# Attention scores of a head pair in two tied half-array runs instead of three, and the mask of batch 1 by VectorE

## The chip, the core and the metric

The kernel runs on one core of one Trainium2 chip. TensorE (PE in the profile) multiplies, VectorE (DVE), ScalarE (ACT) and GpSimd (POOL) do the rest, SyncE (SP) issues the transfers. The metric is the device time of one execution in microseconds, the median of several runs. PE can be used as one array of 128 rows, or as two halves of 64 rows that work at the same time on different operands; a *half-array run* is here a stretch of matmuls of 64 rows with no matmul of 128 rows in between.

## What is computed

Block-causal attention, then a mixture with a maximum of three products, then a second mixture of four experts:

```python
# q, k, v: (4, 8, 576, 64) fp32
scores = scale * np.matmul(q, k.transpose(0, 1, 3, 2))
mask = block_i >= block_j                 # blocks of 64 positions
scores = np.where(mask, scores, -1000000000.0)
scores = scores - np.max(scores, axis=-1, keepdims=True)
attn = np.exp(scores)
attn = attn / (np.sum(attn, axis=-1, keepdims=True) + 1e-09)
attn_out = np.matmul(attn, v)
...
h = np.maximum(np.maximum(x @ w1, x @ w2), x @ w3)
x = h @ w_out                             # 2304 x 512, 768 wide inside
...
out += p[:, e:e + 1] * (np.maximum(x @ w1[e], 0.0) @ w2[e])
```

## The kernel before

**Pairs.** The 4 x 8 heads are worked on as 16 pairs, `n` = 0 to 15; a batch is four pairs (`NPAIR` = 4). The two heads of a pair lie in the lower and the upper 64 partitions of `qs` and `ks`, so one head's scores are a matmul of 64 rows in one half of the array. The 576 query rows of a head are four tiles of 128 rows (`i` = 0 to 3), which need 128, 256, 384 and 512 key columns under the block mask, and 64 tail rows; the tail rows of both heads are made together by full 128-row matmuls over 576 columns (line 161).

**Scores in three steps.** `scores(n, step)` makes tiles i = 0 and 2 for both heads (128 and 384 columns), then i = 3 (512), then i = 1 (256) with the tail rows. The products are fp32; the trace shows each as two records. Score tiles `st` are in PSUM: from `ps_x`, four tiles of one bank (512 columns), which transposes (`tt`), the row weights (`rt`) and, from batch 1 on, the attention values (`pv`) use too, and from `ps_c`, one tile of two banks. In steps 0 and 1 every head has a tile of `ps_x`, in step 2 one of `ps_x` and the one of `ps_c`.

**After the product.** The last 64 columns of a tile are masked for its lower 64 rows: in batches 0 and 1 (`masked = n < 2 * NPAIR`) by a small bf16 matmul of `corner` added to each score tile (line 153), in batches 2 and 3 by a memset on VectorE (line 169). Then VectorE takes the row minimum (scores are kept negated; line 173), ScalarE the exponential with row sums (line 180), VectorE the reciprocals, GpSimd the multiplication with them. `turn_probs` transposes the probabilities on PE (line 241), ScalarE and VectorE copy them out, and `values32` (batch 0) or `values` (batches 1 to 3) multiplies them with v.

**What sets the order.** In each iteration `n` of the main loop the parts of attention of pair `n` and the score steps of pair `n + 1` stand in one list (`todo`), and after each part `filler.upto` puts in products of the first mixture of the batch before (`moe1`, line 493), as many as the part's place in the list asks for: `at = (n + (m + 1) / len(todo)) / NPAIR`. That filler exists from batch 1 on. In batch 0 ScalarE, VectorE and GpSimd convert the weights of the first mixture (lines 418 to 440) besides. The program is then ordered by a scheduler that works with a simulated time; an instruction may move ahead of others on its engine unless `tc.keep_in_program_order` pins it behind the one written before it on the same engine. Before, every half-array matmul of a step is pinned but the first:

```python
                if todo[0] or m:
                    tc.keep_in_program_order(ins)
```

The two full matmuls for the tail rows (line 161) are not pinned.

Of the kernel before, what the change touches and what calls it, by code (L numbers as in the profile page):

```python
# [6 lines left out]
F32 = mybir.dt.float32  # L7
# [4 lines left out]
ACTF = mybir.ActivationFunctionType  # L12
ALU = mybir.AluOpType
AX = mybir.AxisListType
# [6 lines left out]
P = 128  # L21
# [5 lines left out]
def program(tc, q, k, v, w123, w_out, probs, e_w1, e_w2, out):  # L27
    nc = tc.nc
# [7 lines left out]
    NPAIR = H // 2  # L36
# [68 lines left out]
    def prep_pair(n):  # L105
# [15 lines left out]
        (("x", 512), ("x", 512), [(0, 0, 0, P), (2, P, P, 384)]),  # L121
        (("x", 512), ("x", 512), [(3, 0, 0, 512)]),
        (("x", 512), ("c", 1024), [(1, 0, 768, 256)]),
    ]
    COLS = (0, 4, 6, 9)

    def scores(n, step):
        pair = pairs[n]
        if step == 0:
# [6 lines left out]
        masked = n < 2 * NPAIR  # L136
        st = [
            (ps_x if tag == "x" else ps_c).tile([P, cols], F32, name="st", tag=tag) for tag, cols in STEPS[step][0:2]
        ]
        plan = STEPS[step][2]  # L140
        turn = (0, 1) if step == 2 else (1, 0)
        todo = [[], []]
        for i, *at, w in plan:
            views = [st[h][:, at[h]:at[h] + w] for h in range(2)]
            for m, h in enumerate(turn):
                ins = nc.tensor.matmul(  # L146
                    out=views[h], lhsT=qs[own[h], P * i:P * i + P], rhs=ks[own[h], 0:w], start=True, stop=not masked,
                )
                if todo[0] or m:
                    tc.keep_in_program_order(ins)  # L150
            for h in range(2):
                if masked:
                    tc.keep_in_program_order(nc.tensor.matmul(  # L153
                        out=views[h][:, w - 64:w], lhsT=corner[own[h]], rhs=corner[own[h], 0:64],
                        start=False, stop=True,
                    ))
                todo[h].append((i, h, views[h]))
        if step == 2:
            view = st[1][:, 192:768]
            for c, n_ in ((0, 320), (320, 256)):  # L160
                nc.tensor.matmul(  # L161
                    out=view[:, c:c + n_], lhsT=qs[:, QT:QW], rhs=ks[:, c:c + n_], start=True, stop=True
                )
            todo[1].append((4, 0, view))
        col, done = COLS[step], []
        for work in todo:
            for i, h, x in work:
                if i < 4 and not masked:
                    nc.vector.memset(x[lo, x.shape[1] - 64:], 1e30)
            cols = range(col, col + len(work))  # L170
            col += len(work)
            for c, (i, h, x) in zip(cols, work):
                nc.vector.tensor_reduce(mn[:, c:c + 1], x, axis=AX.X, op=ALU.min)  # L173
            for c, (i, h, x) in zip(cols, work):
# [3 lines left out]
                else:  # L178
                    pair["p"][h][i] = to
                exps.append(nc.scalar.activation(  # L180
                    to, x, ACTF.Exp, bias=mn[:, c:c + 1], scale=-1.0, accum_out=sm[:, c:c + 1],
                ))
                done.append((c, i, to))

        def normalise():
# [3 lines left out]
            if n < NPAIR:  # L189

                if step == 0:
                    o = 4 * n * P
                    pair["rb"] = arena[:, o:o + 4 * P].rearrange("p (i h c) -> p i h c", i=4, h=2)
                    to = pair["rb"][:, 0:2].rearrange("p i h c -> p h i c")
                    rs = sm[:, cs].rearrange("p (h i) -> p h i", h=2).unsqueeze(3).to_broadcast([P, 2, 2, 64])
                else:
                    to = pair["rb"][:, step + 1]
                    rs = sm[:, COLS[step]:COLS[step] + 2].unsqueeze(2).to_broadcast([P, 2, 64])
# [387 lines left out]
    stage(scores, 0, 2)  # L586
    for n in range(NALL):
# [7 lines left out]
        s0, s1, s2 = [(scores, n + 1, i) if n + 1 < NALL else (None,) for i in range(3)]  # L595
        pp = (next, prep, None)
        todo = [ta[0], s0, tb[0], s1, va[0], pp, vb[0], ta[1], s2, tb[1], va[1], pp, vb[1]]
# [737 lines left out]
```

## Time and profile before

| | |
|---|---|
| median of 3 runs | 1249.12 us (1248.59 to 1250.19) |
| the profiled execution | 1248.74 us, its span 1247.0 us |
| PE busy | 1223.0 us (98%), 7369 matmul records |
| DVE, ACT, POOL busy | 888.0, 484.6, 332.4 us |
| mean granted clock of PE | 0.995 of full speed |
| half-array score matmuls (line 146) | 256 records, first at 5.0 us, last at 396.2 us |
| corner matmuls (line 153) | 64 records, last at 156.8 us |

Times in the trace are counted from the start of the span. The stretches are: batch 0 up to the first product of the first mixture (83 us), attention of batches 1 to 3 with those products in between (to some 430 us), the rest of the first mixture (to 519 us), the second mixture. The busy time of PE runs from a matmul's start to its modelled end, and matmuls overlap in the pipeline, so it doesn't show what a matmul costs; the distance from one start to the next does.

### The profile page before, as it was taken

The numbers are of one execution on the slowest core, as the hardware profiler recorded it, in microseconds if no ns is written. First come the engines' busy times: TensorE is split into PE (matmuls) and PEld (weight loads), VectorE is DVE, ScalarE is ACT, GpSimd is POOL, SyncE is SP. The second block draws the span as 40 slices with busy tenths as digits, with TensorE's granted clock in tenths as the row PEclk, the third lists the DMA queues.
The fourth block names the chain that finished last, engine by engine and source line by source line (L and its number), as shares of the span: only waits on it lengthen the run. The fifth ranks groups of instructions, "written<-read, shape, count | busy, mean of one in ns | idle before, by whom it ended". The sixth has DMA issues, their size and how long they took to land.

```text
span 1247.0 us, 19462 instructions
## 1 busy us (share of the span) xinstructions
PE 1223.0 (98%) x7369; PEld 1140.3 (91%) x7369; DVE 888.0 (71%) x1636; ACT 484.6 (39%) x1027; POOL 332.4 (27%) x408
## 2 busy tenths in 40 slices
PE   7899999999999999999999999999999999999998
PEld 4578888999999999989999998999999999999998
DVE  5758787555455464278988896758787788576896
ACT  6866666444433431234444441233232222322232
POOL 4637785444244113233343351000000000000000
PEclk9999999999999999999999999999999999999999
DMA  7724474443433476679887875878788887766754
GB/s 271 258 95 167 158 250 160 147 142 106 139 114 102 120 271 259 202 300 340 311 319 289 303 258 167 280 280 316 291 312 310 309 316 290 255 245 239 253 200 180
DMA packets 82352, 290.74 MB, mean 233 GB/s; under 512 B 8716, under 2 KB 18004, under 8 KB 69204
## 3 DMA queue, kind: packets, MB, share of 16 engines
q1 hardware_dynamic: 82260, 289.51, 65.3%
q8 instruction: 58, 0.95, 0.3%
q14 instruction: 34, 0.28, 0.1%
HBM read 206.34 MB, written 83.14 MB: 232 GB/s over the span
## 4 chain that ended last, share of the span: by engine, by line
PE 84%; DVE 7%; DMA 4%; ACT 2%; POOL 1%; issue 1%; SPq 0%; DVEq 0%; ACTq 0%; POOLq 0%
PE m L846 24%; PE m L493 23%; PE o L1005 17%; PE st L146 3%; PE tt L241 3%; PE pv L350 2%; PE o L928 2%; PE o L932 2%; PE o L931 2%; PE m L1005 2%; DMA t<-in_e_w 2%; PE pv L296 1%; PE st L161 1%; DMA raw<-in_q 1%; DVE w L801 1%
## 5 line engine op out<-in xcount | busy, mean ns | idle before, releaser
L493 PE MATMUL m<-xh,wt 128*128 128x288 f32 x1120 | 245.6, 301 | 0.0
L846 PE MATMUL m<-t,w 128*128 128x384 f32 x1152 | 227.8, 336 | 0.0
L1005 PE MATMUL o<-hx,w 128*128 128x384 f32 x1176 | 226.0, 337 | 0.4 <-DMA w<-kb 0.4
L1005 PEld LDWEIGHTS o<-hx,w 128*128 128x128 f32 x1176 | 207.8, 188 | 0.7 <-PE m L846 0.7
L846 PEld LDWEIGHTS m<-t,w 128*128 128x128 f32 x1152 | 203.4, 188 | 2.5
L493 PEld LDWEIGHTS m<-xh,wt 128*128 128x128 f32 x1120 | 184.6, 188 | 7.2 <-DVE mt L531 3.8
L846 PE MATMUL m<-b,w 128*128 128x384 f32 x864 | 175.0, 336 | 1.9 <-ACT tmp L871 1.9
L493 PE MATMUL m<-xl,wt 128*128 128x288 f32 x560 | 165.7, 296 | 0.0
L846 PEld LDWEIGHTS m<-b,w 128*128 128x128 f32 x864 | 153.2, 188 | 5.2 <-ACT tmp L871 2.2
L493 PEld LDWEIGHTS m<-xl,wt 128*128 128x128 f32 x560 | 105.3, 188 | 1.9 <-issue 1.5
L180 ACT ACTIVATE p<-st,mn 128x128 f32<-128x128 f32 (+2 forms) x144 | 78.3, 552 | 53.1 <-DVE mn L173 52.7
L866 DVE TENSOR_TENSOR tmp<-m,tmp 128x384 f32<-128x384 f32 x144 | 77.9, 550 | 19.5 <-PE m L846 19.4
L203 POOL TENSOR_SCALAR p<-p,sm 128x128 f32<-128x128 f32 (+4 forms) x112 | 67.3, 617 | 91.4 <-DVE sm L188 84.1
L493 PE MATMUL m<-hh,wo 128*128 128x288 f32 x384 | 84.1, 304 | 2.3 <-DMA wo<-held 2.1
L976 ACT CAST hx<-hq 128x768 fp32r<-128x768 f32 x49 | 40.6, 837 | 99.0 <-PE o L1005 75.9
L173 DVE TENSOR_REDUCE mn<-st 128x1 f32<-128x128 f32 (+2 forms) x144 | 68.5, 514 | 13.3 <-PE st L153 9.9
L531 DVE TENSOR_TENSOR mt<-m,mt 128x288 f32<-128x288 f32 x96 | 43.4, 454 | 47.7 <-PE m L493 47.1
L928 PE MATMUL o<-w,hh 128*128 128x512 f32 x192 | 74.7, 391 | 0.6 <-ACT hh L906 0.5
L931 PE MATMUL o<-w,hh 128*128 128x512 f32 x192 | 74.6, 390 | 0.0
L932 PE MATMUL o<-w,hl 128*128 128x512 f32 x192 | 74.4, 391 | 0.0
L801 POOL TENSOR_TENSOR w<-part,w 128x512 fp32r<-128x512 f32 x32 | 50.4, 1599 | 89.0 <-ACT w L799 67.1
L241 PE MATMUL tt<-ident,p 128*128 128x128 f32 x400 | 63.6, 281 | 5.0 <-DVE xf L325 2.0
(160 smaller groups left out, 2067.2 us busy)
## 6 DMA issues: line engine op xcount, KB each, us to landing
w<-kb SPq DMA_DIRECT2D x55, 1024.0 KB, 6.0
w<-ka SPq DMA_DIRECT2D x30, 1792.0 KB, 7.7
ka<-w SPq DMA_DIRECT2D x16, 1792.0 KB, 6.7
wt<-held SPq DMA_DIRECT2D x54, 512.0 KB, 4.0
kb<-part SPq DMA_DIRECT2D x16, 1024.0 KB, 6.9
kb<-w SPq DMA_DIRECT2D x16, 768.0 KB, 4.9
arena<-in_w SPq DMA_DIRECT2D x18, 512.0 KB, 4.2
wo<-held SPq DMA_DIRECT2D x12, 768.0 KB, 4.6
```

Source lines behind the costliest of these rows:

```text
L173: nc.vector.tensor_reduce(mn[:, c:c + 1], x, axis=AX.X, op=ALU.min)
L180: exps.append(nc.scalar.activation(to, x, ACTF.Exp, bias=mn[:, c:c + 1], scale=-1.0, accum_out=sm[:, c:c + 1],))
L203: nc.gpsimd.tensor_scalar(x, x, sm[:, c:c + 1], 1.0, op0=ALU.mult, op1=ALU.mult)
L241: nc.tensor.transpose(tt[:, c:c + P], pt[i][:, k0:k0 + P], ident)
L493: nc.tensor.matmul(out=out_, lhsT=w, rhs=x, start=m == 0, stop=m == n - 1)
L801: eng.tensor_tensor(w[:, a:b, 1], raw[:, a:b], f(w[:, a:b, 0]), op=ALU.subtract)
L846: ins = nc.tensor.matmul(out=m, lhsT=a, rhs=b, start=start and n == 0, stop=stop and n == 3 * KH - 1, skip_group_check=True,)
L866: nc.vector.tensor_tensor(t, x, y, op=ALU.add)
L928: ins = nc.tensor.matmul(out=o, lhsT=hh[:, ts], rhs=wh, start=i == 0, stop=False)
L931: nc.tensor.matmul(out=o, lhsT=hh[:, ts], rhs=wl, start=False, stop=False)
L932: nc.tensor.matmul(out=o, lhsT=hl[:, ts], rhs=wh, start=False, stop=i == G - 1)
L1005: nc.tensor.matmul(out=o, lhsT=a, rhs=b, start=start and m == 0, stop=stop and m == 2, skip_group_check=True,)
```

## The change

The steps are two: tiles i = 0 and 2 as before, then i = 3, i = 1 and the tail rows in one. The second step takes three tiles of `ps_x` and the one of `ps_c`. Every matmul of a step is pinned, the first one and the two for the tail rows too. Minimum and exponential go by two tiles at a time in the order of the products, where they went by head; the row sums stand in that order too, so the copy of the row weights in batch 0 is of 4 columns in both steps. In the main loop the second step stands behind the first half's values (`vb[0]`), where step 1 stood behind `tb[0]` and step 2 behind `ta[1]`; the list has 12 parts where it had 13. The corner matmul is left for batch 0 alone; batch 1 (`n` = 4 to 7) is masked by VectorE's memset, as batches 2 and 3 are.

```diff
--- before.py
+++ after.py
@@ -118,11 +118,10 @@
 
 
     STEPS = [
-        (("x", 512), ("x", 512), [(0, 0, 0, P), (2, P, P, 384)]),
-        (("x", 512), ("x", 512), [(3, 0, 0, 512)]),
-        (("x", 512), ("c", 1024), [(1, 0, 768, 256)]),
+        [(0, 0, P, (0, 1)), (2, P, 384, (0, 1))],
+        [(3, 0, 512, (0, 1)), (1, (0, 768), 256, (2, 3))],
     ]
-    COLS = (0, 4, 6, 9)
+    COLS = (0, 4, 9)
 
     def scores(n, step):
         pair = pairs[n]
@@ -133,54 +132,53 @@
                 sm=ap_.tile([P, COLS[-1], 2], F32, name="sm", tag="sm", bufs=2),
             )
         mn, sm, qs, ks = pair["mn"], pair["sm"][:, :, 0], pair["qs"], pair["ks"]
-        masked = n < 2 * NPAIR
+        masked = n < NPAIR
         st = [
-            (ps_x if tag == "x" else ps_c).tile([P, cols], F32, name="st", tag=tag) for tag, cols in STEPS[step][0:2]
+            (ps_c if m == 3 else ps_x).tile([P, 1024 if m == 3 else 512], F32, name="st", tag="c" if m == 3 else "x")
+            for m in range((2, 4)[step])
         ]
-        plan = STEPS[step][2]
-        turn = (0, 1) if step == 2 else (1, 0)
-        todo = [[], []]
-        for i, *at, w in plan:
-            views = [st[h][:, at[h]:at[h] + w] for h in range(2)]
-            for m, h in enumerate(turn):
-                ins = nc.tensor.matmul(
+        todo = []
+        for i, at, w, tiles_ in STEPS[step]:
+            views = []
+            for h in range(2):
+                o = at if isinstance(at, int) else at[h]
+                views.append(st[tiles_[h]][:, o:o + w])
+            for h in (1, 0):
+                tc.keep_in_program_order(nc.tensor.matmul(
                     out=views[h], lhsT=qs[own[h], P * i:P * i + P], rhs=ks[own[h], 0:w], start=True, stop=not masked,
-                )
-                if todo[0] or m:
-                    tc.keep_in_program_order(ins)
+                ))
             for h in range(2):
                 if masked:
                     tc.keep_in_program_order(nc.tensor.matmul(
                         out=views[h][:, w - 64:w], lhsT=corner[own[h]], rhs=corner[own[h], 0:64],
                         start=False, stop=True,
                     ))
-                todo[h].append((i, h, views[h]))
-        if step == 2:
-            view = st[1][:, 192:768]
+                todo.append((i, h, views[h]))
+        if step == 1:
+            view = st[3][:, 192:768]
             for c, n_ in ((0, 320), (320, 256)):
-                nc.tensor.matmul(
+                tc.keep_in_program_order(nc.tensor.matmul(
                     out=view[:, c:c + n_], lhsT=qs[:, QT:QW], rhs=ks[:, c:c + n_], start=True, stop=True
-                )
-            todo[1].append((4, 0, view))
-        col, done = COLS[step], []
-        for work in todo:
-            for i, h, x in work:
+                ))
+            todo.append((4, 0, view))
+        done, cols = [], list(range(COLS[step], COLS[step + 1]))
+        for c in (0, 2, 4):
+            work = list(zip(cols, todo))[c:c + 2]
+            for _, (i, h, x) in work:
                 if i < 4 and not masked:
                     nc.vector.memset(x[lo, x.shape[1] - 64:], 1e30)
-            cols = range(col, col + len(work))
-            col += len(work)
-            for c, (i, h, x) in zip(cols, work):
-                nc.vector.tensor_reduce(mn[:, c:c + 1], x, axis=AX.X, op=ALU.min)
-            for c, (i, h, x) in zip(cols, work):
+            for m, (i, h, x) in work:
+                nc.vector.tensor_reduce(mn[:, m:m + 1], x, axis=AX.X, op=ALU.min)
+            for m, (i, h, x) in work:
                 to = ap_.tile([P, x.shape[1]], F32, name=f"p{i}", tag=f"p{i}", bufs=2 if i == 4 else 3)
                 if i == 4:
                     pair["p4"] = to
                 else:
                     pair["p"][h][i] = to
                 exps.append(nc.scalar.activation(
-                    to, x, ACTF.Exp, bias=mn[:, c:c + 1], scale=-1.0, accum_out=sm[:, c:c + 1],
+                    to, x, ACTF.Exp, bias=mn[:, m:m + 1], scale=-1.0, accum_out=sm[:, m:m + 1],
                 ))
-                done.append((c, i, to))
+                done.append((m, i, to))
 
         def normalise():
             cs = slice(COLS[step], COLS[step + 1])
@@ -191,11 +189,8 @@
                 if step == 0:
                     o = 4 * n * P
                     pair["rb"] = arena[:, o:o + 4 * P].rearrange("p (i h c) -> p i h c", i=4, h=2)
-                    to = pair["rb"][:, 0:2].rearrange("p i h c -> p h i c")
-                    rs = sm[:, cs].rearrange("p (h i) -> p h i", h=2).unsqueeze(3).to_broadcast([P, 2, 2, 64])
-                else:
-                    to = pair["rb"][:, step + 1]
-                    rs = sm[:, COLS[step]:COLS[step] + 2].unsqueeze(2).to_broadcast([P, 2, 64])
+                to = pair["rb"][:, 2 * step:2 * step + 2].rearrange("p i h c -> p (i h) c")
+                rs = sm[:, COLS[step]:COLS[step] + 4].unsqueeze(2).to_broadcast([P, 4, 64])
                 nc.gpsimd.tensor_copy(to, rs)
             for c, i, x in done:
                 if n < NPAIR and i < 4:
@@ -583,7 +578,6 @@
     stage(scores, 0, 0)
     stage(scores, 0, 1)
     stage(all_of, prep_pair(1))
-    stage(scores, 0, 2)
     for n in range(NALL):
         b, d = divmod(n, NPAIR)
         ahead = n + 2 < NALL
@@ -592,9 +586,9 @@
         ta, tb, va, vb = [
             [(fn, g + h, part) for h in range(2)] for fn in (turn_probs, values) for part in range(2)
         ]
-        s0, s1, s2 = [(scores, n + 1, i) if n + 1 < NALL else (None,) for i in range(3)]
+        s0, s1 = [(scores, n + 1, i) if n + 1 < NALL else (None,) for i in range(2)]
         pp = (next, prep, None)
-        todo = [ta[0], s0, tb[0], s1, va[0], pp, vb[0], ta[1], s2, tb[1], va[1], pp, vb[1]]
+        todo = [ta[0], s0, tb[0], va[0], pp, vb[0], s1, ta[1], tb[1], va[1], pp, vb[1]]
         for m, st in enumerate(todo):
             if d == NPAIR - 1 and m == 7:
                 moe1_inputs(b, range(KD - 1))
```

In the rows below, `st` are score tiles, `tt` transposed probabilities, `pv` values, `m` the products of the first mixture, `p_...` tiles of probabilities; x2 stands for both heads. Line 146 of before is line 147 after, 161 is 160, 493 is 488, 180 is 178, 418 and 419 are 413 and 414, 241 is 236.

PE before, in batches 2 and 3, step 1 of a pair among products of the first mixture:

```order
L493 MATMUL m<-xl,wt 128x288
L493 MATMUL m<-xh,wt 128x288
L146 MATMUL st<-raw 128x512 x2
L493 MATMUL m<-xh,wt 128x288
L493 MATMUL m<-xl,wt 128x288
```

The run of 512 columns stands alone, with products of the first mixture on both sides. PE before, step 2 of the same pair, some 40 rows on:

```order
L493 MATMUL m<-hh,wo 128x288
L146 MATMUL st<-raw 128x256 x2
L161 MATMUL st<-raw 128x320
L161 MATMUL st<-raw 128x256
L493 MATMUL m<-hh,wo 128x288
```

The 256 columns are a run of their own, followed by the tail rows. PE after, the second step at the same place of the program:

```order
L488 MATMUL m<-hl,wo 128x288
L488 MATMUL m<-hh,wo 128x288
L147 MATMUL st<-raw 128x512 x2
L147 MATMUL st<-raw 128x256 x2
L160 MATMUL st<-raw 128x320
L160 MATMUL st<-raw 128x256
L488 MATMUL m<-hh,wo 128x288
```

Both runs have become one, with the tail rows behind it. PE before, step 0 of a pair in the same batches, whose first matmul is not pinned:

```order
L241 MATMUL tt<-ident,p_3155 128x128
L241 MATMUL tt<-ident,p_3157 128x128 x2
L146 MATMUL st<-raw 128x128
L493 MATMUL m<-xh,wt 128x288
L493 MATMUL m<-xl,wt 128x288
```

One head's 128 columns stand alone; 17 rows on follow the other head's 128 and both heads' 384. PE after, step 0:

```order
L488 MATMUL m<-xl,wt 128x288
L488 MATMUL m<-xh,wt 128x288
L147 MATMUL st<-raw 128x128 x2
L147 MATMUL st<-raw 128x384 x2
L236 MATMUL tt<-ident,p_3289 128x128 x2
```

All four matmuls of the step stand together there. ScalarE before, at the start of the program, with the exponentials of pair 0 (128 columns: i = 0, 384: i = 2, 512: i = 3; p_157 and p_159 are the first head's) and the conversion of weights:

```order
L180 ACT_TABLE_LOAD
L180 ACTIVATE p_157,sm<-st,mn 128x128
L180 ACTIVATE p_159,sm<-st,mn 128x384
L418 ACTIVATE arena<-arena 128x512
L419 ACTIVATE arena<-arena 128x512
L180 ACTIVATE p_163,sm<-st,mn 128x128
L180 ACTIVATE p_165,sm<-st,mn 128x384
```

The first head's two exponentials come first. ScalarE after, the same place (p_157 and p_163 are the first head's):

```order
L178 ACT_TABLE_LOAD
L178 ACTIVATE p_157,sm<-st,mn 128x128
L413 ACTIVATE arena<-arena 128x512
L414 ACTIVATE arena<-arena 128x512
L178 ACTIVATE p_159,sm<-st,mn 128x128
L178 ACTIVATE p_163,sm<-st,mn 128x384
L178 ACTIVATE p_165,sm<-st,mn 128x384
```

The conversion of a weight piece and the second head's 128 columns now stand ahead of the first head's 384 columns.

## Rows read from the trace of the kernel before

**Rows 1.** Busy time by stretch: start:end, length, then PE, PEld, DVE, ACT, POOL busy.

```profile
15.79:83.03 67.24, 59.61 (x318) 39.30 (x317) 47.69 (x101) 53.09 (x151) 37.61 (x49) 0.95 0.59 200
83.03:412.00 328.97, 328.08 (x2301) 295.49 (x2301) 212.15 (x541) 170.07 (x449) 173.64 (x252) 1.00 0.46 146
```

**Rows 2.** Waits of PE from 83 to 412 us: total us, times, longest.

```profile
PE st L146 <- DVE eh L269: 0.7, 1, 0.7
```

**Rows 3.** PE in order of time, 512-column run: start, us, then instruction.

```profile
386.39 0.29 PE L493 MATMUL m<-xh,wt 128*128 128x288 f32 x1
386.61 1.13 PE L146 MATMUL st<-raw 64*128 64x512 f32 x4
387.67 0.40 PE L493 MATMUL m<-xh,wt 128*128 128x288 f32 x1
387.91 0.29 PE L493 MATMUL m<-xl,wt 128*128 128x288 f32 x1
388.04 0.43 PE L493 MATMUL m<-xh,wt 128*128 128x288 f32 x2
```

**Rows 4.** PE in order of time, tied run of 128 and 384 columns.

```profile
167.83 1.14 PE L146 MATMUL st<-raw 64*128 64x128 f32 x8
168.90 0.44 PE L241 MATMUL tt<-ident,p 128*128 128x128 f32 x2
```

**Rows 5.** PE in order of time, 256-column run and the tail rows.

```profile
395.87 0.70 PE L146 MATMUL st<-raw 64*128 64x256 f32 x4
396.50 1.24 PE L161 MATMUL st<-raw 128*128 128x320 f32 x4
```

**Rows 6.** PE in order of time, a lone 128-column matmul and its partner's run.

```profile
226.96 0.49 PE L146 MATMUL st<-raw 64*128 64x128 f32 x2
227.37 0.40 PE L493 MATMUL m<-xh,wt 128*128 128x288 f32 x1
...
230.75 1.13 PE L146 MATMUL st<-raw 64*128 64x128 f32 x6
231.81 0.44 PE L241 MATMUL tt<-ident,p 128*128 128x128 f32 x2
```

**Rows 7.** PE in order of time, one head's 512 columns alone.

```profile
174.60 1.12 PE L146 MATMUL st<-raw 64*128 64x512 f32 x2
175.65 0.40 PE L493 MATMUL m<-xh,wt 128*128 128x288 f32 x1
```

**Rows 8.** PE in order of time, runs with corners.

```profile
67.97 0.49 PE L146 MATMUL st<-raw 64*128 64x128 f32 x4
...
69.17 1.15 PE L241 MATMUL tt<-ident,p 128*128 128x128 f32 x6
...
72.53 1.13 PE L146 MATMUL st<-raw 64*128 64x512 f32 x4
...
73.62 0.65 PE L322 MATMUL rt<-ident,arena 128*128 128x128 f32 x4
```

**Rows 9.** PE in order of time, batch 0, with the wait in brackets.

```profile
75.28 0.66 PE L241 MATMUL tt<-ident,p 128*128 128x128 f32 x4 [0.57 <-ACT p L180]
```

**Rows 10.** ACT, then PE, in order of time, pair 0.

```profile
10.47 0.66 ACT L418 ACTIVATE arena<-arena 128x512 f32<-128x512 f32 x1
...
11.56 0.38 ACT L180 ACTIVATE p<-st,mn 128x128 f32<-128x128 f32 x1
...
10.63 1.22 PE L146 MATMUL st<-raw 64*128 64x256 f32 x4 [1.32 <-ACT p L180]
```

**Rows 11.** The memsets of batches 2 and 3: ns min/median/max, first and last start.

```profile
L169 DVE MEMSET st<- x64: 112/112/112, 170.6 to 397.8; 64x64 f32 x64
```

**Rows 12.** PE in order of time, end of the first mixture.

```profile
508.43 0.57 PE L493 MATMUL m<-hh,wo 128*128 128x288 f32 x1 [2.10 <-DMA wo<-held]
508.79 0.44 PE L493 MATMUL m<-hl,wo 128*128 128x288 f32 x1
509.03 0.68 PE L493 MATMUL m<-hh,wo 128*128 128x288 f32 x2
```

## Prediction

> **What bounds the kernel now.** I read the busy time by stretch first [rows 1]. From 83.03 to 412 us TensorE (PE) is busy for 328.08 of 328.97 us: this is the stretch where attention of batches 1 to 3 is threaded through the products of the first mixture, whose matmuls fill every gap. VectorE is busy for 212.15 us of it. PE's longest wait there is 0.7 us [rows 2]. So in this stretch a microsecond of PE saved is a microsecond saved, as long as nobody starts to wait. Earlier, from 15.79 to 83.03, PE works 59.61 of 67.24 us and ScalarE 53.09: no filler exists yet, and the end is a chain through PE, VectorE and ScalarE. The end of the first mixture and all of the second come after 412 us; the change doesn't touch their code.
>
> "Busy" hides the cost I am after, so the next view is PE's order in time, and in it the starts, not the durations. Filler products start 0.13 us apart (387.91 to 388.04) [rows 3]. Around a run of 64-row matmuls (two heads, one in each half of the array, started together) this is broken twice: 0.22 us from the last filler's start to the run's (386.39 to 386.61), and 0.24 us from the first filler after the run to the second (387.67 to 387.91). That is 0.09 + 0.11 us of entry and exit. The run itself lasts 1.06 us for two heads of 512 columns, and 0.63 us for two heads of 256 [rows 5]. The difference, 0.43 us, is what 256 columns cost; so 512 columns cost 0.86, and 0.20 us of every run is fixed. So the fixed price of a run is 0.09 + 0.20 + 0.11 = 0.40 us.
>
> Does a second pair of matmuls in the same run pay again? A run of 128 and 384 columns for both heads, tied, with no corners, lasts 1.07 us (167.83 to 168.90) [rows 4]: the same 512 columns as in rows 3, at the same length. A second pair adds its columns only.
>
> **The change, part by part.** Counting runs in the order of both programs: 60 before, 39 after. Up to the first filler 15 before and 12 after; from there on 45 and 27.
>
> Merging. For 11 pairs in the filled stretch the 512-column run and the 256-column run become one: 11 x 0.40 = 4.4 us. The full-array products of the 64 tail rows follow the 256 columns before and after, so that edge stays.
>
> Lone 128-column matmuls. Only the first matmul of a step was free to move before, and the scheduler put it early, as a run of its own: 0.41 us from its start to the next filler (226.96 to 227.37) [rows 6], with an exit as in rows 3; with entry and exit 0.09 + 0.41 + 0.11 = 0.61 us. Its partner's run gains nothing by that: 1.06 us (230.75 to 231.81), as a full one. There are 9 of these in the filled stretch before and 2 after: 7 x 0.61 = 4.3 us.
>
> Lone 512s and a lone 256. One head's 512 columns alone take 1.05 us [rows 7], as long as both heads together, so a split costs 0.09 + 1.05 + 0.11 = 1.25 us. Three before, two after: 1.25 us won. After has one new split, of 256 columns: 0.40 + 0.43 = 0.83 us lost.
>
> Corner matmuls of batch 1. With corners the 128 + 384 run lasts 1.20 us (67.97 to 69.17) against 1.07, and the 512 run 1.09 (72.53 to 73.62) against 1.06 [rows 8]. Taking 0.03 for the 256 run as well, 0.19 us a pair; three pairs lie in the filled stretch: 0.6 us. What replaces them is a memset of 0.11 us on VectorE for each of 8 tiles [rows 11], 32 in all, 3.6 us against over 100 us that VectorE is idle there. It lies between the matmul and the row minimum, so the exponential comes about 0.2 us later per two tiles; PE runs filler meanwhile.
>
> Sum for the filled stretch: 4.4 + 4.3 + 1.25 - 0.83 + 0.6 = 9.7 us.
>
> Before the filler. Four merges at 0.3 to 0.4 (there corners stand between the pairs, so some of the fixed part may return), one more lone 128 (-0.6) and one pair without corners (+0.2) are about 1.0 us of PE, on a chain that PE doesn't bound alone. Against it stands ScalarE at the very start. The 256-column run of pair 0 starts at 10.63, when two exponentials have released its bank. The order now puts two weight-conversion instructions (1.09 us, from 10.47 to 11.56) and one more 128-column exponential (0.38 us) ahead of that release [rows 10]: some 1.5 us later, with PE idle. The conversion is work that is owed anyway, so part of it comes back. Net I take 0.4 us lost, bounds 2 us won and 3.5 us lost.
>
> New waits. The merged step takes three of the four one-bank tiles at once, and transposes and values use the same four. Before, in batch 0, a second transpose group waits 0.57 us for an exponential to free its bank, 2.75 us after the 512 run began (72.53 to 75.28) [rows 9]. After, 256 columns (0.43 us), the 576 tail columns (about 1.0 at the same price a column) and one transpose group (about 0.4) lie between that run's end and the second group, 2.9 us from its start without any filler; in the filled stretch mostly 12 fillers or more (1.6 us) come on top. I take 0.7 us in all, bounds 0 and 3.
>
> Total: 9.7 - 0.4 - 0.7 = 8.6 us. The profiled execution took 1248.74 us (its span 1247.0 and 1.7 around it): 1240.1. The median of the runs shown is 0.4 above it: 1240.5 us.
>
> [...] Rows 4 show the fixed 0.20 paid once for two pairs. [...]
>
> **Rivals.** That the ties don't hold is no rival: the order after still shows eight split runs (five lone 128s, two lone 512s, one lone 256), and all are in the counts above.
> B. Every weight load inside a run shows. Then the merged 256 columns pay their fixed 0.20 again and a merge saves only entry and exit, 0.20: the sum loses 2.2 us, 1242.7. Against it is the 1.07 of rows 4; for it, that no run of before puts 256 columns behind 512.
> C. Batch 0 takes it back. PE that has idled runs slower for a while: after the 2.10 us wait that ends at 508.43 fillers start 0.24 us apart (508.79 to 509.03) in place of 0.13 [rows 12], half the pace. The later start of pair 0 and a spell or two at half pace would cost 4 us more than I took: 1244.5.
> D. Slower, by banks: the transposes behind every merged run wait for the exponentials of its tiles. That begins where the release comes later than the cover just worked out, so where the queues of VectorE and ScalarE add 0.2 us in batch 0, and 1.7 us in the filled stretch. To end slower the 15 merged runs must lose more than the 9.3 us that are won without this term and 2.5 us more, 0.79 us each, against the 0.57 of rows 9; at 0.85 us each, 12.7 us: 1252.5. Against it: nearly no wait of PE in the filled stretch now [rows 2].
> E. The change doesn't reach the end. The load of the last output weights of the first mixture is awaited for 2.10 us [rows 12]. If that load's time is fixed by the transfer queue and not by PE, all that PE gains waits there: 1249.1. Against it: the buffer is freed by PE's own products, which move with it.
> F. Batch 0 gains and that wait goes too: 2.4 + 2.1 us more, 1236.0.
>
> **How the numbers follow.** Forecast 0.62, B 0.10, C 0.10, D 0.05, E 0.05, F 0.08. The likeliest is 1240.5. Its own bounds (new waits, batch 0) are 1237 to 1243.5; to leave out no more than 2 in 10 the range takes in B, C and F: 1235.5 to 1246. The measurement tells 0.2%, 2.5 us, from no change. Faster: forecast, B, F and most of C, 0.88; same: E and a little of C, 0.07; slower: D, 0.05.
>
> **What would show it.** In the trace after: a merged run of 512 and 256 columns that lasts 1.06 + 0.43 = 1.49 us (right) or 1.69 (B); the stretch from the first filler product to the last product of attention about 9 us shorter; PE's waits in it below 3 us (D if 8 or more); pair 0's 256-column run near 12.1 instead of 10.63. I am wrong if PE there isn't full any more, or if the stretch shrinks and the end doesn't.

## The result, and the profile of the changed kernel

The changed kernel takes 1258.34 us (median of 6 runs, 1256.37 to 1260.54), the kernel before 1249.73 us beside it (6 runs, 1248.59 to 1252.11): a ratio of 1.0068, 95% interval 1.0053 to 1.0082. It is slower, where 1240.5 us was forecast; the time lies 12 us above the range. The profiled execution after took 1257.09 us, its span 1255.3.

Busy time of the kernel after by stretch, with the columns of [rows 1]; the first stretch now ends at the first filler product, at 91.71 us:

```profile
15.79:91.71 75.92, 61.74 (x300) 40.38 (x298) 48.48 (x100) 53.55 (x152) 38.17 (x47) 0.89 0.54 178
91.71:420.00 328.29, 320.75 (x2266) 293.19 (x2266) 214.57 (x541) 167.72 (x447) 170.93 (x250) 0.99 0.46 145
```

Against [rows 1] two things changed. PE is no longer full in the filled stretch: 7.5 us of 328.29 are not busy, where 0.9 were not. And the stretch before the filler is 8.3 us longer (83.44 to 91.71), with a mean granted clock of 0.89 in place of 0.95. From the first filler product to the last product of attention both kernels need 347.1 us (83.4 to 430.5, and 91.7 to 438.8). So the 9.7 us that the sum promised there have gone to something else, and batch 0 has lost 8.3 on top. That is the whole result: what comes behind it moves by less than 2 us in either direction (the wait of [rows 12] shrinks from 2.1 to 1.3 us, two waits for weights in the second mixture grow).

The products themselves do what was forecast. PE of the kernel after in order of time, the merged run of a pair in batch 2 and the start of the next pair's:

```profile
285.62 1.56 PE L147 MATMUL st<-raw 64*128 64x512 f32 x8
287.11 1.24 PE L160 MATMUL st<-raw 128*128 128x320 f32 x4
...
314.43 1.56 PE L147 MATMUL st<-raw 64*128 64x512 f32 x8
```

A run of 512 and 256 columns lasts from its start to that of the tail rows, 285.62 to 287.11 = 1.49 us. From pair to pair there are 28.81 us (285.62 to 314.43, with 144 filler products in between). Before it was 29.81 us with the same 144, as the starts of the tail rows show:

```profile
277.20 1.24 PE L161 MATMUL st<-raw 128*128 128x320 f32 x4
...
307.01 1.24 PE L161 MATMUL st<-raw 128*128 128x320 f32 x4
```

One microsecond a pair is 0.40 for a merge and 0.61 for a lone 128, as in the sum. It holds from pair 10 on (between pairs 9 and 10 it is 0.7). Everything goes wrong ahead of them.

**Where the filled stretch gives it back.** Waits of PE in the kernel after from 91.71 to 420 us (total us, times, longest), to be set against the single 0.7 of [rows 2]:

```profile
PE tt L236 <- DVE eh L264: 2.8, 1, 2.8
PE pv L334 <- DVE eh L255: 1.4, 1, 1.4
PE tt L236 <- DVE st L169: 1.4, 1, 1.4
PE m L488 <- DVE mt L526: 0.9, 2, 0.5
PE tt L236 <- ACT p L178: 0.8, 1, 0.8
PE m L488 <- ACT mt L524: 0.2, 1, 0.2
```

Their sum is 7.5 us, all ahead of 219 us, and 6.5 of it is a wait for VectorE. The 2.8 us wait is followed by 3.41 us at a granted clock of 0.50 (row below), which by an estimate from that figure takes another 1.7: 9.2 us in all, 8.5 more than before, of the 9.7 us. They are not spread over batch 1: the four longest lie between the tail rows of pair 8 and those of pair 9,

```profile
191.43 1.24 PE L160 MATMUL st<-raw 128*128 128x320 f32 x4
...
229.19 1.24 PE L160 MATMUL st<-raw 128*128 128x320 f32 x4
```

which are 37.8 us apart, where they were 30.3 apart before with as many filler products (144) in between. The longest wait, as PE and then as VectorE saw it:

```profile
212.94 0.82 PE L236 MATMUL tt<-ident,p 128*128 128x128 f32 x6
216.53 0.33 PE L236 MATMUL tt<-ident,p 128*128 128x128 f32 x1 [2.77 <-DVE eh L264]
```

```profile
211.73 0.47 DVE L421 TENSOR_SCALAR arena<-arena 128x384 uint32<-128x384 uint32 x1
212.23 1.80 DVE L422 SCALAR_TENSOR_TENSOR arena<-arena 128x384 uint32<-128x384 uint32 x1
214.04 0.11 DVE L169 MEMSET st<- 64x64 f32 x1
214.07 1.43 DVE L507 TENSOR_TENSOR xl<-xf,xh 128x576 fp32r<-128x576 f32 x1
215.42 0.28 DVE L171 TENSOR_REDUCE mn<-st 128x1 f32<-128x128 f32 x1
215.71 0.11 DVE L169 MEMSET st<- 64x64 f32 x1
215.85 0.29 DVE L171 TENSOR_REDUCE mn<-st 128x1 f32<-128x128 f32 x1
216.06 0.41 DVE L264 TENSOR_TENSOR eh<-tt,eh 128x256 fp32r<-128x256 f32 x1
```

VectorE never idles there. The subtraction that PE waits for (line 264) stands in its queue behind two conversion instructions, the low half of the mixture's input (line 507), two memsets and two row minima. In these rows each instruction begins within 0.1 us of the end of the one before it, so what is late in one of them is late in all. A transpose reads probabilities and doesn't read what line 264 writes: by the program, what it waits for is one of the four one-bank tiles, which that subtraction has yet to read.

**Where batch 0 loses.** Waits of PE in the kernel after from 5.2 to 91.71 us, the longest four beside the first load's 5.1:

```profile
PE tt L236 <- ACT p L178: 3.6, 4, 1.5
PE pv L283 <- ACT eh L261: 3.5, 2, 2.6
PE tt L236 <- DVE eh L261: 3.0, 2, 2.7
PE pv L291 <- ACT eh L261: 2.7, 1, 2.7
```

All waits there but that first one make 15.2 us, against 8.7 in the kernel before. The start of pair 0, which the sum had 1.5 us later, is not late: its 256-column run starts at 9.17, stands still once,

```profile
10.82 0.48 PE L147 MATMUL st<-raw 64*128 64x256 f32 x1 [0.76 <-ACT p L178]
```

and the tail rows behind it come at 11.47, where they came at 11.83 before. What is late comes after it. ScalarE and PE of the kernel after, in order of time:

```profile
14.40 0.19 ACT L178 ACTIVATION_READ_ACCUMULATOR p<-st,mn 128x1 f32 x1
17.10 0.66 ACT L414 ACTIVATE arena<-arena 128x512 int32<-128x512 uint32 x1 [2.52 <-POOL arena L426]
17.67 0.61 ACT L89 CAST wt<-arena 128x512 fp32r<-128x512 f32 x1
18.18 0.47 ACT L178 ACTIVATE p<-st,mn 128x256 f32<-128x256 f32 x1
...
18.64 0.57 ACT L261 COPY eh<-tt 128x512 f32<-128x512 f32 x1
...
19.26 0.49 PE L283 MATMUL pv<-eh,vraw 128*128 128x128 f32 x2 [2.58 <-ACT eh L261]
...
22.45 2.93 PE L291 MATMUL pv<-eh,vraw 128*128 128x384 f32 x4 [2.70 <-ACT eh L261]
```

From 14.59 to 17.10 ScalarE stands still on a conversion instruction (line 414) that waits for GpSimd, whose own queue stands behind a late load (POOL raw L107 waited for raw<-in_q until 14.75). An exponential and a copy that PE needs come behind it in ScalarE's queue. PE waits 2.58 us, then 2.70 us more behind the next such group, and works at a granted clock of 0.50 afterwards (first window below). These rows show how a conversion instruction holds up what stands behind it; they aren't the whole loss. In the kernel before, ScalarE idled 2.50 us at the same place, for a row minimum, and PE's first product with v came at the same time:

```profile
19.28 0.49 PE L288 MATMUL pv<-eh,vraw 128*128 128x128 f32 x2 [0.82 <-ACT eh L266]
```

At the tail rows of pair 1 the kernel after is 0.8 us behind (28.07 before, 28.84 after), at those of pair 2 it is 3.6 (45.70 and 49.27). In between lies the 2.7 us wait for VectorE, whose copy (line 261) stands behind two conversion instructions, the first of which had waited 2.25 us for GpSimd:

```profile
41.22 0.69 PE L236 MATMUL tt<-ident,p 128*128 128x128 f32 x2 [2.68 <-DVE eh L261]
```

Windows of the kernel after, columns as in [rows 1]; the eighth figure is the granted clock:

```profile
19.87:26.69 6.82, 4.24 (x10) 2.85 (x11) 5.26 (x13) 5.19 (x16) 4.99 (x7) 0.50 0.76 256
40.35:47.17 6.82, 5.95 (x18) 4.56 (x19) 3.54 (x7) 5.09 (x16) 5.36 (x5) 0.50 0.59 191
217.84:221.25 3.41, 3.01 (x10) 2.81 (x11) 3.07 (x9) 2.65 (x9) 1.59 (x2) 0.50 0.21 77
```

Each of these stretches begins during or within 2 us of a wait of PE for ScalarE or VectorE. With a third one from 84.7 to 88.1 that is 17 us at half the clock before the filler, against 6.8 in the kernel before. In the stretch from 217.84 us on filler products start 0.24 us apart (218.62 to 218.86), where they start 0.13 apart in [rows 3].

### The profile page after: what moved, and what is told of

It is laid out like the page before. It is cut to its first block, busy times and chain, and to the rows that moved or that the text cites. A ratio compares the mean times of both kernels' runs of the same rounds, so it can differ in the third digit from the quotient of the medians.

```text
span 1255.3 us, 19381 instructions
## 1 busy us (share of the span) xinstructions
PE 1217.5 (97%) x7337; PEld 1138.8 (91%) x7337; DVE 890.4 (71%) x1636; ACT 483.5 (39%) x1027; POOL 330.3 (26%) x404
## 4 chain that ended last, share of the span: by engine, by line
PE 84%; DMA 5%; DVE 4%; POOL 3%; ACT 3%; issue 2%; SPq 0%; DVEq 0%; ACTq 0%; POOLq 0%
PE m L840 25%; PE m L488 21%; PE o L999 16%; PE o L922 3%; PE o L926 3%; PE o L925 3%; PE tt L236 2%; PE st L147 2%; PE pv L345 2%; PE m L999 2%; PE pv L291 2%; DMA raw<-in_q 1%; DMA w<-kb 1%; DMA kb<-part 1%; PE st L160 1%
## 5 line engine op out<-in xcount | busy, mean ns | idle before, releaser
L171 DVE TENSOR_REDUCE mn<-st 128x1 f32<-128x128 f32 (+2 forms) x144 | 72.4, 514 | 21.7 <-ACT p L178 16.1
```

The costliest lines, as they stand in the source:

```text
L171: nc.vector.tensor_reduce(mn[:, m:m + 1], x, axis=AX.X, op=ALU.min)
```

## Experiments

Three theories stood after this reading. **1**: batch 0 loses by the place of the weight conversion in ScalarE's queue (1a), or by the merged step itself (1b). **2**, later **A**: the mask of batch 1 costs, because VectorE converts weights there and has no room. **3**: the banks, the prediction's rival D. All ratios are to the kernel before, run beside each.

**The mask alone, the merge alone.** In the kernel before:

```
-        masked = n < 2 * NPAIR
+        masked = n < NPAIR
```

> The kernel before (three steps), with batch 1's corners written by VectorE. Theory 1 (the new order of batch 0 and the merged step beside the weight conversion cost the time): the mask is nearly free, PE wins about 0.19 us for each of 4 pairs and 32 memsets of 0.11 us fall on a VectorE that is 80% busy there, so 1248.5 to 1251, against 1249.7 before. Theory 2 (the memsets on a busy VectorE cost the time of batch 1): 3 us or more slower, 1253 or above. Theory 3 (PSUM banks): as theory 1.

Measured: 1.0030 (1.0016 to 1.0044), median 1254.54 against 1250.67. In the kernel after the same line put back:

```
-        masked = n < NPAIR
+        masked = n < 2 * NPAIR
```

> The kernel after (two tied steps), with batch 1's corners on TensorE again. Theory 1: within 1.5 us of the kernel after, 1257 to 1260. Theory 2: most of the loss of batch 1 comes back, 1252 or below. Theory 3: as theory 1.

Measured: 0.9996 (0.9983 to 1.0009), median 1248.94. Its 12 runs lie between 1246.88 and 1254.26, and its profiled one (1253.79) is among the longest. So the mask costs 0.30% with three steps and 0.72% (9 us) with two. I had held theory 1 alone and expected next to nothing of it; theory 2 was the right one for batch 1. The stretch from the first filler product to the last of attention says the same in the traces: 347.1 us before, 351.4 with the mask alone, 340.8 with the merge alone, 347.1 with both.

**Two steps from some pair on.** Both forms of `scores` in one kernel, and

```
+        merged = n + 1 >= 5        # 9, 1 in the others
```

> Three steps for pairs 0 to 4 and two tied steps from pair 5 on, corners in batches 0 and 1; the order of batch 0 is that of before. Theory 1: the 8.3 us of batch 0 are not lost (first filler product at 83.5), pairs 9 to 15 win 1.0 us each, and pairs 5 to 8 lose up to 7: 1243 to 1250, in any case 8 us or more below the kernel after. If batch 0 is not what matters and the loss is in the merged step wherever it stands (theory 3, banks): 1254 or above.

> Three steps for pairs 0 to 8 and two tied steps from pair 9 on (after the weight conversion is over), corners in batches 0 and 1. Theory 1 (a run costs 0.40 us beside its columns, and nothing waits where VectorE, ScalarE and GpSimd have no conversion): 7 pairs at 1.0 us, 1242 to 1243.5. Theory 3 (banks): the merged step waits in every pair and wins less than half of it, 1246.5 or above.

> Three steps for pair 0 alone and two tied steps from pair 1 on, corners in batches 0 and 1. At the start of the program ScalarE keeps the order of before: both first-head exponentials of pair 0 ahead of the weight conversion. If what batch 0 loses is that start (theory 1a), this is as good as two steps from pair 5 on: 1245.5 to 1248. If the merged step beside the conversion in pairs 1 to 4 loses it (theory 1b), it is no better than two steps everywhere with corners: 1248.5 to 1251.

Measured: from 5 on 0.9973 (0.9960 to 0.9986), from 9 on 0.9959 (0.9943 to 0.9975), from 1 on 0.9999 (0.9985 to 1.0013). From 9 on it is 1244.91, a little short of what was expected, and theory 3, a wait for banks wherever the merged step stands, is refuted: from 222 to 420 us, with no conversion beside it, PE has no wait at all. The stretch is 341.2 us from 5 on and 341.0 from 9 on: merging pairs 5 to 8 gives nothing that these runs show. From 1 on is no better than everywhere (0.9996), so the start of pair 0 isn't all of batch 0's loss; its first filler product comes at 87.0 us, about half way.

**Is it the memset itself?** In the kernel before, for batches 2 and 3:

```
-                    nc.vector.memset(x[lo, x.shape[1] - 64:], 1e30)
+                    for _ in range(2):
+                        nc.vector.memset(x[lo, x.shape[1] - 64:], 1e30)
```

> The kernel before with every memset of batches 2 and 3 written twice: 64 memsets more on VectorE, 0.11 us each and about 0.2 with the gap behind it, 7 to 13 us of VectorE's time. Theory A (the mask of batch 1 costs time because VectorE, which converts weights there, has no room): batches 2 and 3 have room, so no change, within 1 us of before. Rival B (a memset costs wherever it stands, since it lies between product and exponential): 3 us or more slower.

Measured: 1.0001 (0.9991 to 1.0011). 64 memsets more cost nothing where VectorE has room. Then room was made in batch 1:

```
+            au, high = au[:, 0:16], high[:, 0:16]
             nc.vector.tensor_scalar(au, au, 3, None, op0=ALU.logical_shift_left)
             nc.vector.scalar_tensor_tensor(
                 au, high, 0x80000000, au, op0=ALU.bitwise_and, op1=ALU.bitwise_xor
             )
```

> The kernel before with two of VectorE's three instructions for a piece of weights (the shift and the combination of sign bits) made 16 columns wide instead of 512, which leaves most of the conversion out: the output is not the reference's. It is the partner of the next run. Theory A: little to win in itself, since PE hardly waits in batch 1 of before: 1 to 4 us faster than before by batch 0.

> The same with batch 1's corners by VectorE: it leaves the same conversion out. Theory A: with some 1.2 us less of VectorE's work for each of 18 pieces in batch 1, the 32 memsets have room, and the mask costs nothing or wins the 0.6 us of the corner matmuls: from 1 us faster to 1 us slower than the partner, where without the cut it cost 3.8. Rival B, or an order that the scheduler makes worse: 3 us or more slower than the partner.

Measured: 1.0003 (0.9991 to 1.0015) with corners and 0.9965 (0.9951 to 0.9978) with the mask by VectorE. With room the mask wins 0.4%, without it loses 0.3%. PE is full in both traces; of the one with the mask:

```profile
84.00:225.00 141.00, 141.00 (x984) 126.59 (x984) 108.63 (x282) 90.42 (x229) 94.00 (x131) 1.00 0.55 181
```

Theory A holds in sign. That the whole is so much faster was not expected. The profiled execution with the mask is among the shortest of its twelve (1241.86), 8.9 us of span below its partner's; of these, 3.6 lie in the filled stretch (342.9 against 346.5), 1.6 ahead of it and 3.0 at the end of the first mixture, where the wait of [rows 12] is 0.7 in place of 2.2 us. The corner matmuls were priced at 0.6. So an order changed by the cut moves microseconds by itself.

**Batch 0: the conversion held back.** In the kernel after with corners (and, as a partner, in the kernel before):

```
-            with tc.issue_after(exps[3 * i].ins) if i < 2 else nullcontext():
+            with tc.issue_after(exps[(3, 8)[i]].ins) if i < 2 else nullcontext():
...
-            rounded(nc.scalar, high, a)
+            with tc.issue_after(exps[9 + 4 * i].ins) if i < 6 else nullcontext():
+                rounded(nc.scalar, high, a)
```

> Two tied steps everywhere, corners in batches 0 and 1, and the first pieces of the weight conversion held back on ScalarE: the first two pieces behind the fourth and the ninth exponential of pair 0, the rounding copies of the first six behind exponentials of pairs 1 to 3. If batch 0 loses its 7 to 8 us because the conversion stands ahead of pair 0's and pair 1's exponentials and copies (theory 1a), the first filler product comes at 87.5 or earlier in place of 91.2, and the whole is 2 to 5 us below the 1248.9 of two steps with corners. If the merged step itself loses it, by its banks and by exponentials that come in a bunch (theory 1b), the first filler is at 89.5 or later and the whole at 1248 or above.

> The kernel before with the same two constraints on the weight conversion: the partner of the run ahead. In its own order they nearly hold already, so within 1.5 us of before under either theory; if it wins as much as the merged one does, what the constraint is worth has nothing to do with the merged step.

Measured: 0.9951 (0.9939 to 0.9963), 1245.73 us, where the same kernel without the constraint had 0.9996; the partner 1.0005 (0.9996 to 1.0015). PE's first filler product without the constraint, then with it:

```profile
91.22 0.40 PE L488 MATMUL m<-xh,wt 128*128 128x288 f32 x1
```

```profile
84.36 0.40 PE L489 MATMUL m<-xh,wt 128*128 128x288 f32 x1
```

So 1a is shown: the merged steps lose nothing to speak of in batch 0 (84.4 against 83.4 before) once the conversion stands behind the exponentials, and the constraint is worth 0.45%, 5.6 us, to the merged kernel and nothing to the one before. In the traces the half-clock time before the filler goes from 17 us to 6.8, but the 17 are those of that one run of 1253.79 us, 4.9 above its median. Rival 1b, which the run from pair 1 on had favoured, falls; that in that run pairs 1 to 4 had the trouble of 1a too would fit, and was not tested.

**How the mask's price grows.** First doubled in the kernel after, for batch 1 alone:

```
+                    for _ in range(2 if n < 2 * NPAIR else 1):
                         nc.vector.memset(x[lo, x.shape[1] - 64:], 1e30)
```

> The kernel after with the 32 memsets of batch 1 written twice. Theory A (VectorE has no room in batch 1): 32 times some 0.2 us are 6.4 us of a VectorE that sets the pace there, so 3 to 9 us slower than the kernel after, 1261 to 1267. If the mask's cost there was an accident of the order: within 2 us of the kernel after, 1256.5 to 1260.

Measured: 1.0039 (1.0026 to 1.0051), 1257.22: by the ratios 0.3% below the kernel after, not above it. Its filled stretch is 349.8 us, 2.7 longer, but its first filler product came at 87.3, 4.4 earlier. Theory A's number for it is refuted, and the rival's range, that of an accident of the order, holds the time. Then on the kernel with the conversion held back, where batch 0 disturbs less: all four pairs of batch 1 by VectorE, and pairs 6 and 7 alone (`masked = n < 6`).

> The kernel after with the weight conversion held back on ScalarE as in the run with corners and two steps everywhere (1245.7). The loss of batch 0 and that of the mask are separate if this lies by the mask's price above that run and by the pin's below the kernel after: 1250 to 1254.5. If the mask's price was only a matter of how batch 0's order had pushed the conversion back, it is within 2 us of the run with corners: 1244 to 1248.

> The same, but VectorE masks pairs 6 and 7 alone, pairs 4 and 5 keep their corners: 16 memsets instead of 32. If the price goes by the number of memsets, half of it: 1248 to 1250. If VectorE only falls behind near the end of batch 1, where the conversion, the inputs of the mixture and pair 8's attention come together, all of it: 1250 to 1254.

Measured: no pair by VectorE 0.9951, two pairs 0.9973 (0.9964 to 0.9983), four pairs 1.0015 (1.0004 to 1.0027). The four cost 0.64%, 8 us; the two a third of it by these medians. Batch 0's and the mask's loss are separate. The traces don't bear out a price by the memset: the filled stretch is 341.2, 347.4 and 349.2 us, so two masked pairs lengthen it by 6.3 of the 8.0 us that four do, and the execution with two got some 4 back behind it. With four, most of the loss sits in one place, between the tail rows of pairs 8 and 9: 39.0 us apart, where they are 31.8 apart with none. Last, room for VectorE in the kernel after itself, by the same cut as above:

> The kernel after with two of VectorE's three instructions for a piece of weights made 16 columns wide instead of 512: it leaves most of the conversion out, and its output is not the reference's. Theory A (the mask costs because VectorE has no room beside the conversion): the stretch from the first filler product to the last product of attention shrinks from 347.1 to 341 or less, PE's waits in batch 1 go below 2 us, and the whole is 6 us or more below the kernel after: 1252 or less. If a memset between product and exponential is what costs: stretch 345 or more, the whole 1255 or above.

Measured: 0.9956 (0.9943 to 0.9969), 1245.77 us: 1.1% below the kernel after. The stretch is 338.8 us in place of 347.1. PE's waits from 89.5 to 420 us:

```profile
PE m L489 <- ACT arena L538: 0.7, 1, 0.7
PE m L489 <- DVE mt L527: 0.7, 1, 0.7
PE pv L334 <- ACT p L178: 0.6, 1, 0.6
PE m L489 <- ACT mt L525: 0.2, 1, 0.2
PE tt L236 <- POOL p L198: 0.2, 1, 0.2
```

2.4 us in place of 7.5, and none above 0.7: all three waits for VectorE at the top of the list are gone. VectorE's load is lower; the kernel after, then this one, up to 220 us, the fifth figure with its count being VectorE's:

```profile
91.71:220.00 128.29, 120.75 (x820) 107.14 (x820) 106.76 (x244) 81.06 (x207) 88.57 (x114) 0.99 0.51 171
```

```profile
89.56:220.00 130.44, 127.93 (x886) 114.56 (x886) 98.76 (x253) 82.47 (x212) 84.73 (x118) 1.00 0.54 180
```

106.76 of 128.29 us is 83%, 98.76 of 130.44 is 76%. The share by itself doesn't tell the two apart: from the first filler product to 220 us it is 78% both with the conversion held back and no masked pair, which costs nothing, and with two masked pairs, which cost 6.3 us of that stretch. The rows of the longest wait point to what stands ahead of the instruction that PE waits for.

**Ties alone, and the better version.** In the kernel before, nothing but:

```
-                if todo[0] or m:
-                    tc.keep_in_program_order(ins)
+                tc.keep_in_program_order(ins)
```

> Three steps for all pairs, as before, with every half-array matmul pinned, the first one of a step too: 54 runs in place of 60, no merge, no mask, no other list. By the price of a lone 128 (0.61 us) in each of pairs 9 to 15, 4.3 us there, and 1.5 us in pairs 5 to 8: 1243.5 to 1246. If a tie makes PE wait for a bank that the free matmul did not need: within 2 us of before.

Measured: 0.9944 (0.9931 to 0.9957), 1245.57 us. The filled stretch is 4.4 us shorter (342.7), where 5.8 were expected; where the rest of the 0.56% lies isn't shown. The starts of two pairs' 256-column runs are 29.18 us apart, 0.63 less than before:

```profile
244.56 0.70 PE L146 MATMUL st<-raw 64*128 64x256 f32 x4
...
273.74 0.70 PE L146 MATMUL st<-raw 64*128 64x256 f32 x4
```

And with two steps from pair 9 on besides:

> Three steps for pairs 0 to 8 with every half-array matmul pinned, the first one of a step too, two tied steps from pair 9 on, corners in batches 0 and 1. By the price of a run (0.40 us and a lone 128 at 0.61) the ties of pairs 5 to 8 win 2 to 3 us of PE more than two steps from pair 9 on alone, which took 1244.9: 1241.5 to 1243.5. If batch 1 takes back what PE gains there, since VectorE sets its pace: 1244 to 1246.

Measured: 0.9930 (0.9918 to 0.9942), 1243.38 us against 1251.81 beside it. It beats both kernels: by the ratios 0.7% below the one before and 1.4% below the one after. Its filled stretch is 339.5 us, and its first filler product comes at 82.6.

## Why the prediction was wrong

**The price of a run: right.** The merged run lasts 1.49 us, to the hundredth. Rival B, which had 1.69 by supposing that every weight load inside a run shows, is refuted. Ties win 0.63 us a pair (29.81 to 29.18) and the merge 0.37 more (to 28.81), against 0.61 and 0.40 in the sum. That PE was full there, so that PE saved is time saved, was right from pair 9 on. With room made on VectorE the whole filled stretch is 8.3 us shorter than before (338.8), with 2.4 us of waits left in it: the 9.7 us of the sum are about what PE's own work lost.

**The step that failed first: one mean over two stages.** The prediction set 3.6 us of memsets "against over 100 us that VectorE is idle there", and found PE running filler meanwhile. The 100 us are a mean from 83 to 412 us [rows 1]. Split where the conversion ends, the kernel before shows:

```profile
83.45:217.60 134.15, 133.26 (x931) 117.89 (x930) 106.03 (x241) 86.43 (x219) 93.49 (x121) 1.00 0.53 175
217.60:397.40 179.80, 179.80 (x1261) 162.81 (x1259) 98.24 (x280) 77.05 (x213) 74.83 (x121) 1.00 0.41 125
```

VectorE is 79% busy up to 217.6 us and 55% behind it. The memsets of the change went into the first part alone, where its idle times in the kernel before are mostly waits for ScalarE (15.7 of 28.1 us) and PE (7.3 us) in its own chains. There the mask didn't win 0.6 us but cost 8 to 9 with two steps (3.9 with three). PE running filler meanwhile was no cover: the transpose of the longest wait stood ahead of the next filler products in PE's order, and PE stood still. The new waits (0.7 us, bounds 0 and 3) came to 7.5, mostly this same term: the longest is for a bank, as that term supposed, but for one that VectorE's queue kept, not an exponential. With the corners back on TensorE 2.8 us of waits remain, four times the 0.7, so the merged step beside the conversion has a share in it.

**The second: batch 0.** The sum took 0.4 us net, bounds 2 won and 3.5 lost; it was 8.3 in the profiled execution, and some 6 by the runs with and without the held-back conversion (0.45% with the corners, 0.53% with the mask). The order of ScalarE had been seen, and the conversion in it [rows 10]. It was priced by the durations of what now stands ahead, 1.09 + 0.38 us, at the start of pair 0, and just there nothing was lost: the tail rows of pair 0 came 0.4 us earlier than before. What the runs show is that the conversion's place ahead of the exponentials of pairs 0 to 3 costs; the rows show how, by conversion instructions that wait themselves (2.52 us for GpSimd on ScalarE, 2.25 on VectorE) with exponentials and copies behind them. How much each of these waits costs isn't shown. Rival C had one half of it, the spells at half the clock (17 us in place of 6.8); its other half, the later start of pair 0, didn't come.

**The rivals.** D, the only slower one, had the sign and a part of the cause: banks that come free late because of a queue. It had them kept by the exponentials of the merged run, and for those transposes waited 0.8 us in the filled stretch and 3.6 us in batch 0; the longest wait is behind the first step's run, for VectorE's subtraction. E falls by the runs that gained: in the fastest version the load of [rows 12] is still awaited for 2.0 us, and the gain reaches the end. No rival said that VectorE's queue would hold PE up in one batch, the first thing that "the mask is written by VectorE" should have raised. Slower at 0.05 was far too little for a change that puts work on VectorE and reorders ScalarE where both convert weights.

**What stays open.** That the mask costs only beside the conversion is shown by the runs that leave most of VectorE's share of it out; that it costs because VectorE has no room is argued. Why two masked pairs cost 3 us and four cost 8, and why memsets written twice lengthened the stretch by 2.7 us only, isn't settled: every added instruction also changes the order around it, and that most of the cost with four masked pairs sits in one place near the end of batch 1 doesn't look like a price for each memset. Nor was it tried whether the conversion could be moved off VectorE, which would show whether the mask can pay at all here.

## What to carry to other kernels

Before work is put on an engine "that has room", read its busy share in the very stage where the work lands, split the stretch wherever another stream of work ends, and look at what stands ahead of the instructions that the busiest engine waits for: the share alone didn't tell here. When an order moves an instruction ahead in an engine's queue, ask what that instruction waits for, and not only what it takes. And price the parts of a change apart: here one line, the tie of the first matmul, was worth 0.56%, the merge behind the conversion added 0.14%, and the two parts that met the conversion cost more than both.

## What the runs showed of the hardware

In the kernel after, VectorE's combination of sign bits (line 422) took 543 to 1801 ns:

```profile
L422 DVE SCALAR_TENSOR_TENSOR arena<-arena x17: 543/774/1801, 106.1 to 212.2; 128x512 uint32<-128x512 uint32 x9, 128x384 uint32<-128x384 uint32 x8
```

```profile
L526 DVE TENSOR_TENSOR mt<-m,mt x24: 428/448/459, 99.8 to 188.3; 128x288 f32<-128x288 f32 x24
```

These two groups give ns min/median/max, the first and last start and the forms. Five of the 17 combinations ran while GpSimd ran nothing: 668 to 682 ns for 512 columns, 543 and 560 for 384. The twelve that had a GpSimd instruction beside them took 732 to 1643 and 654 to 1801. The 1801 ns are those of 212.23 above, when GpSimd ran a subtraction:

```profile
211.94 1.68 POOL L115 TENSOR_TENSOR vs<-vraw,vs 128x640 fp32r<-128x640 f32 x1
```

GpSimd beside it doesn't always go with a longer one: in the kernel before, 15 of the 17 combinations from 84 to 215 us ran beside it and took 553 to 1296 ns, and six of the nine of 512 columns took 673 to 691. Line 526 stays between 428 and 459 ns, with GpSimd beside 19 of its 24. Why the combination is longer in some places was not tested by a run of its own. Its mean from 84 to 215 us was 738 ns in the kernel before and 929 in the kernel after, 12.6 and 15.8 us in all for 17 of them, so VectorE had 3.2 us less room for anything else in batch 1 after.
